# Top-32 attention with a highway layer behind it: the first pair of score tiles handled one tile at a time, and the order of the last instructions changed

## The chip, the cores and the metric

The kernel runs on one core of a Trainium2 chip. The metric is the device time of one execution in microseconds (us), as the median of several runs. The kernel before takes 830.66 us (five runs, 830.6 to 831.35).

## What is computed

For 8 batches and 8 heads, 576 queries meet 576 keys of width 64; each row of scores keeps its 32 largest, takes a softmax over them and weighs the values with it. The result goes through a highway layer of width 512.

```python
scores = scale * np.matmul(q, k.transpose(0, 1, 3, 2))
kth = np.partition(scores, -top_k, axis=-1)[..., -top_k:-top_k + 1]
scores = np.where(scores >= kth, scores, -1000000000.0)
attn = np.exp(scores - np.max(scores, axis=-1, keepdims=True))
x = np.matmul(attn / np.sum(attn, axis=-1, keepdims=True), v)   # then heads side by side: 4608 x 512
H = np.maximum(x @ w_h, 0.0)
T = 1.0 / (1.0 + np.exp(-(x @ w_t + b_t)))
return T * H + (1.0 - T) * x
```

## The kernel before

**Unit of work.** A tile is 128 query rows of one head by all 576 keys. Two tiles make a pair (a normal pair is the two heads 2i and 2i+1 of one block of queries), four pairs make a group (all heads of 128 queries), and 144 pairs make the kernel. The main loop (line 1016) takes one step `n` per pair; instructions are issued in the order in which they are written (the `Pinned` wrappers keep it), on PE (TensorE), DVE (VectorE), ACT (ScalarE), POOL (GpSimd) and the DMA queue of SP (SyncE). Since all instructions pass through those wrappers, the profile gives nearly all of them line 38, and they are told apart by the tiles that they write and read.

**One pair, from scores to output.** `scores` (line 222) multiplies queries by keys in fp32 into the PSUM tile `ps` of two tiles by 1024 columns. Columns 0 to 511 and 512 to 575 are separate products, and the products of the pair's two tiles alternate: tile 0 and tile 1 for the first 512 columns, then both for the last 64. The queries and keys of an even head lie in rows 0 to 63 of `kq`, those of an odd head in rows 64 to 127. There is one `ps`, so the scores of pair n+1 can be written only when the readers of pair n are through. `evac` (line 244) lets ACT write max(score, 0) of both tiles in one instruction of 1152 columns into an SBUF buffer (`zfirst` for pair 0, parts of `z0` to `z2` for the others). `tree` (line 255) has DVE fold the two halves of each row by a maximum into `hi`: for pairs 0 and 1 from the SBUF copy alone, later from `ps` and the copy, so that DVE then holds `ps` until it has read it. `folds` (line 275) folds on, into `hh`, `h3` and `w2`, `minima` (line 298) makes the folded-away smaller halves (DVE for pair 0, POOL for the others), and `lists`, `tops` and `rest` find the 32nd value of each row by rounds of MAX8 (eight largest) and MATCH_REPLACE8 (take them out). `run` issues such lists in rounds, one operation of each list per round. Later steps mask, transpose, take the exponential (`parts`), multiply by the values (`av`), and feed the finished group to the highway layer (`ffn_x`, `ffn_h`, `ffn_t` and so on).

**The opening.** Ahead of the loop, eight products of zeros keep PE going (`spin`, line 968). Then come the transposes of the first keys and of the first block of queries (`turn_first(pr, 0, 1)` for the first two heads), the scores of pair 0 and their evacuation, the transposes of the other six heads' first queries (`turn_first(pr, 1, NHP)`), whose copy into `kq` DVE makes (line 155, 384 columns), and the next keys, whose copy ACT makes. In step 0 DVE folds pair 0, and `run(opening, 1)` issues one round of its lists (line 1023). In step 1 PE computes the scores of pair 2, transposes the keys of pair 3, and then makes nine products of zeros (`WARM`, line 25). In step 2 it goes on with the scores of pair 3.

**The end.** After the loop (from line 1113) the last three pairs and the last two groups, `gp` and `gl`, are finished by an order written out by hand. `final_norm` divides the sums of heads by their denominators (DVE: RECIPROCAL into `scales`, then a product into `x`), `final_turn` transposes (PE) and copies to `xT` (DVE), `final_h` and `final_t` multiply by the two weights (PE), and `final_o` makes the last products and stores the two halves of the output (lines 650 to 665). In between stand the steps of the group before: `ffn_gate(gp)` (tanh on ACT), `ffn_e(gp)` (DVE, x times the gate, 512 columns), `ffn_o(gp)` (DVE, adds and stores, 512 columns) and `ffn_d(gl)` (DVE, 512 columns). `judge` looks whether the shortcuts held; a slow exact path behind it is not taken with these inputs.

Of the kernel before, what the change touches and what calls it, by code (L numbers as in the profile page):

```python
# [8 lines left out]
AF = mybir.ActivationFunctionType  # L9
# [12 lines left out]
NZ = 3  # L22
NPEN = 3
IDLE = {11: 3, 10: 8, 9: 3, 3: 3, 2: 3}
WARM = {1: 9, 2: 7, 3: 8}


class Pinned:


    def __init__(self, tc, engine):
        self._tc, self._engine = tc, engine
# [10 lines left out]
class PinnedCore:  # L43
    def __init__(self, tc):
        for name in ("tensor", "vector", "scalar", "gpsimd"):
            setattr(self, name, Pinned(tc, getattr(tc.nc, name)))
        self.sync = tc.nc.sync
        self.queue = Pinned(tc, tc.nc.sync)


class Group:
# [19 lines left out]
class Ops:  # L71


    def __init__(self, ctx, tc, shared, exact):
        self.tc = tc
        self.nc = tc.nc if exact else PinnedCore(tc)
        self.__dict__.update(shared)
        self.exact = exact
        s = "g" if exact else ""

        def pool(name, bufs, **kw):
            return ctx.enter_context(tc.tile_pool(name=name + s, bufs=bufs, **kw))

        PS = bass.MemoryType.PSUM
        self.ldpool = pool("ld", 2 if exact else 3)
        self.kqpool = pool("kq", 1 if exact else 2)
        self.scpool = pool("sc", 2) if exact else None
        self.treepool = pool("tree", 3)
        self.wpool = pool("w", 4)
        self.lpool = pool("l", 2)  # L90
        self.etpool = pool("et", 2)
        self.xpool = pool("x", 2)
        self.fpool = pool("f", 2)
        self.ztps = pool("ztps", 2, space=PS)
        self.zrps = pool("zrps", 1, space=PS)
        self.fps = pool("fps", 1, space=PS)
        self.bigctx = ctx.enter_context(ExitStack())
        self.bigps = self.bigctx.enter_context(
            tc.tile_pool(name="bigps" + s, bufs=1, space=PS)
        )  # L100
        self.st = {}
        self.quads = {}
        self.spare = []

    def load(self, pr, name, hp, eng=None, other=None, c0=0):
        nc, D, P = self.nc, self.D, self.P
# [35 lines left out]
    def turn_first(self, pr, h0, h1):  # L144


        nc, P = self.nc, self.P
        kqps = self.ztps.tile([P, 512], FP32, tag="zt", name="kqps")
        for hp in range(h0, h1):
            nc.tensor.transpose(  # L150
                kqps[:, hp * P : (hp + 1) * P],
                pr["qc"][:, 2 * hp : 2 * hp + 2, :].rearrange("p h d -> p (h d)"),
                self.ident[:],
            )
        nc.vector.tensor_copy(
            pr["kq"][:, 1, h0:h1, 0:P],
            kqps[:, h0 * P : h1 * P].rearrange("p (h q) -> p h q", q=P),
        )
# [63 lines left out]
    def scores(self, n, g, pi, prep):  # L222
        nc, D, S, P = self.nc, self.D, self.S, self.P
        kq = prep["kq"]
        qs = g.qt * P
        ps = self.bigps.tile([P, 2, 1024], FP32, tag="big", name="ps")
        for s0, s1 in ((0, 512), (512, S)):
            for ti, heads in enumerate(g.pairs[pi]):
                for hi, h in enumerate(heads):
                    r = slice((h % 2) * D, (h % 2 + 1) * D)  # L230
                    rows = slice(hi * (P // 2), hi * (P // 2) + g.qlen)
                    nc.tensor.matmul(
                        ps[rows, ti, s0:s1],
                        kq[r, 1, h // 2, qs : qs + g.qlen],
                        kq[r, 0, h // 2, s0:s1],
                    )
        self.st[n] = dict(ps=ps)

    def zview(self, n):
        if n == 0 and not self.exact:  # L240
            return self.zfirst
        return self.zbufs[n // 2 % NZ][:, 2 * (n % 2) : 2 * (n % 2) + 2, :]

    def evac(self, n):
        nc, P, S = self.nc, self.P, self.S
        ps = self.st[n]["ps"]
        if self.exact:
            sc = self.scpool.tile([P, 2, S], FP32, tag="sc", name="sc")
            nc.scalar.copy(sc[:], ps[:, :, 0:S])
        else:  # L250
            sc = self.zview(n)[:, :, 0:S]
            nc.scalar.activation(sc, ps[:, :, 0:S], AF.Relu)
        self.st[n]["sc"] = sc

    def tree(self, n):
        nc, P, S = self.nc, self.P, self.S
        H1, H2, H3 = S // 2, S // 4, S // 8
        k, half = n // 2, slice(2 * (n % 2), 2 * (n % 2) + 2)
        if n % 2 == 0 or n == 1:
            self.quads[n if n < 2 else k + 1] = tuple(  # L260
                self.treepool.tile([P, 4, w], FP32, tag=name, name=name, bufs=bufs)[
                    :, 0 : 2 if n < 2 else 4, :
                ]
                for name, w, bufs in (("hi", H1, 3), ("hh", H2, 3), ("h3", H3, 2))
            )
        ps, sc = self.st[n].pop("ps"), self.st[n]["sc"]
        if n < 2:
            hi, ps = self.quads[n][0], sc
        else:
            hi = self.quads[k + 1][0][:, half, :]  # L270
        nc.vector.tensor_tensor(
            hi[:, 0:2, :], ps[:, :, 0:H1], sc[:, :, H1:S], ALU.max
        )
# [24 lines left out]
    def minima(self, k, after):  # L298


        H1, H2 = self.S // 2, self.S // 4
        gp, S = self.nc.gpsimd, self.S
        hi, hh, h3 = self.quads[k]
        z = self.zview(k) if k < 2 else self.zbufs[(k - 1) % NZ]
        sci, hii, hhi = [a[:].bitcast(I32) for a in (z, hi, hh)]
        if k == 0:
            self.nc.vector.tensor_tensor(
                hi, z[:, :, 0:H1], z[:, :, H1:S], ALU.min
            )
            return  # L310
        if k == 1:
            head = gp.tensor_tensor(hii, sci[:, :, 0:H1], hii, ALU.subtract)
        else:
            head = gp.tensor_tensor(hhi, hii[:, :, 0:H2], hhi, ALU.subtract)
        self.tc.add_manual_dep(
            head.ins,
            after.ins.name,
            mybir.DependencyInfo(
                mybir.DependencyClass.Sync, mybir.DependencyReason.DATA
            ),  # L320
            reason="after the folds",
        )
        if k > 1:
            gp.tensor_tensor(hhi, hhi, hii[:, :, H2:H1], ALU.add)
            gp.tensor_tensor(hii, sci[:, :, 0:H1], hii, ALU.subtract)
        gp.tensor_tensor(hii, hii, sci[:, :, H1:S], ALU.add)
# [476 lines left out]
def kernel(  # L803
# [25 lines left out]
    def const(shape, dt, name):  # L829
        return consts.tile(shape, dt, tag=name, name=name)  # L830
# [8 lines left out]
    for i in range(NZ):  # L839
        zt = const([P, 4, nck * P], FP32, f"z{i}")  # L840
        nc.gpsimd.memset(zt[:, :, S : nck * P], NEG)
        zbufs.append(zt)
    zfirst = const([P, 2, nck * P], FP32, "zfirst")
    nc.gpsimd.memset(zfirst[:, :, S : nck * P], NEG)
    pens = []
    for i in range(NPEN):
        pt = const([P, 2, nck * P], BF16, f"pen{i}")
# [27 lines left out]
    with ExitStack() as cm:  # L875
# [100 lines left out]
        ops.load(pr, "qin", 2, queue, None, 1)  # L976
        ops.scores(0, *pairs[0], preps[0])
        ops.evac(0)
        ops.turn_first(pr, 1, NHP)
        ops.load_rest(pr, "qrest", queue, tag="qc")  # L980
        ops.turn(pr, "kin", 1, True)
# [30 lines left out]
        def values(m):  # L1012
            g, pi = pairs[m]
            ops.av(m, g, pi, preps[g.b]["vb"])

        while step <= NPR:
            n = step
            if have(n):
                ops.tree(n)
                if n < 2:  # L1020
                    ops.minima(n, ops.folds(n, *pairs[n], []))
                    opening += ops.lists(n, *pairs[n])
                    ops.run(opening, 1)
                elif n % 2:
                    nq = n // 2 + 1
                    ops.minima(nq, ops.folds(nq, *pairs[n - 1], fill))
                    fill = []
                if NHP <= n + 1 < 2 * NHP:
                    ops.turn(pr, "qin", n + 1 - NHP, None, 1)
                if n == NHP:  # L1030
                    ops.load(pr, "qin", 3, None, None, 1)
                if n == 2 * NHP:
                    ops.turn_rest(pr, 0, NHP, ("qrest",))
# [122 lines left out]
        part(1)  # L1156
        values(m + 1)
        ops.final_norm(gl, 2, 3)
        ops.ffn_gate(gp)
        ops.ffn_e(gp)  # L1160
        gl.ps = ops.fps.tile([P, 512], FP32, tag="fp", name="hps")
        ops.final_h(gl, 0, 2)
        values(m + 2)
        ops.final_turn(
            gl, 2, 3, ops.ztps.tile([P, 512], FP32, tag="zt", name="xtps")
        )
        ops.final_norm(gl, 3, 4)
        ops.final_t(gl, 0, 2)
        judge(banks[3])
        ops.final_turn(  # L1170
            gl, 3, 4, ops.ztps.tile([P, 512], FP32, tag="zt", name="xtps")
        )
        ops.ffn_o(gp, *out_rows(gp))
        ops.final_h(gl, 2, 3)
        ops.final_t(gl, 2, 3)
# [79 lines left out]
```

## Time and profile before

| | |
|---|---|
| median of five runs | 830.66 us |
| the profiled execution | 831.33 us |
| its span, first to last instruction | 829.6 us |
| DVE busy | 814.7 us |
| ACT busy | 761.6 us |
| PE busy | 710.8 us |
| POOL busy | 710.7 us |
| last instruction of DVE ends | 825.05 us |
| mean granted clock of TensorE | 0.989 |

The profile is that of one execution, and its times count from the start of the span. An instruction's row gives its start, its length, the engine, the tile that it writes and the tile that it reads, and, in brackets, how long the engine had been idle and what ended that. Instructions on one engine overlap a little: a row's length is longer than the distance to the next row. The chain of waits is the work that ended last, followed back from the last instruction.

### The profile page before, as it was taken

What the parts mean: (1) busy time and instruction counts of PE and PEld (TensorE: products, weight loads), DVE (VectorE), ACT (ScalarE), POOL (GpSimd) and SP (SyncE); (2) the same over time, 40 slices, a digit from 0 to 9 for tenths busy, and PEclk for the clock granted to TensorE, in tenths of its full rate; (3) what the DMA queues carried; (4) which work ended last, traced back from release to release, by engine and by line L of the source; (5) the groups of instructions that cost most, each with busy time, mean ns of one, the idle gap of its engine ahead of it and who ended that gap; (6) DMA issues with size and microseconds to landing.
All of it is one profiled execution on the core that took longest, in us unless ns stands there. A gap on an engine that the chain in (4) does not pass through costs nothing.

```text
span 829.6 us, 20251 instructions
## 1 busy us (share of the span) xinstructions
PE 710.8 (86%) x6635; PEld 490.2 (59%) x6635; DVE 814.7 (98%) x4173; ACT 761.6 (92%) x1522; POOL 710.7 (86%) x460
## 2 busy tenths in 40 slices
PE   8788888788898888888888898878988888899986
PEld 4565566565566656665566565656556655565654
DVE  5999999999999999999999999999999999999997
ACT  4899999999999999899999999989999999988985
POOL 5888888798889889978889988888888989887993
PEclk9999999999999999999999999999999999999999
DMA  8564333234254431433325342323413321111222
GB/s 187 131 109 84 65 90 75 61 68 90 38 102 84 77 90 30 75 71 65 90 53 92 70 96 58 64 53 71 112 31 65 52 40 40 40 36 25 45 39 56
DMA packets 105329, 58.40 MB, mean 70 GB/s; under 512 B 82304, under 2 KB 91904, under 8 KB 105216
## 3 DMA queue, kind: packets, MB, share of 16 engines
q1 hardware_dynamic: 93200, 37.47, 17.6%
q0 software_dynamic: 11200, 19.27, 16.2%
q8 instruction: 54, 0.88, 0.4%
q14 instruction: 59, 0.48, 0.2%
q10 hardware_dynamic: 816, 0.30, 0.1%
HBM read 30.67 MB, written 18.35 MB: 59 GB/s over the span
## 4 chain that ended last, share of the span: by engine, by line
DVE 94%; PE 3%; ACT 1%; POOL 1%; issue 0%; POOLq 0%; DVEq 0%
DVE w L38 53%; DVE m L38 20%; DVE hi L38 11%; DVE hh L38 6%; DVE h L38 3%; PE warm L38 1%; PE ps L38 1%; PE zt L38 1%; PE t L38 1%; DVE scales L38 0%; POOL hh L38 0%; ACT pen L38 0%; POOL hi L38 0%; ACT z L38 0%; ACT kq L38 0%
## 5 line engine op out<-in xcount | busy, mean ns | idle before, releaser
L38 PE MATMUL ps<-kq 64*128 64x64 f32 (+3 forms) x1280 | 202.3, 439 | 47.7 <-DVE hi L38 42.4
L38 ACT ACTIVATE pen<-z,m 128x576 bf16<-128x576 f32 x286 | 225.7, 790 | 1.2 <-DVE m L38 1.0
L38 PE MATMUL zt<-ident,z 128*128 128x128 f32 x1140 | 212.5, 280 | 2.0 <-ACT xT L38 2.0
L38 PE MATMUL zt<-nident,pen 128*128 128x128 bf16 x1148 | 205.7, 220 | 0.0
L38 ACT ACTIVATE z<-ps 128x1152 f32<-128x1152 f32 x143 | 161.9, 1132 | 43.1 <-PE ps L38 39.3
L38 POOL TENSOR_TENSOR hi<-z,hi 128x1152 int32<-128x1152 int32 (+1 forms) x72 | 188.3, 2616 | 11.2 <-DVE hh L38 5.6
L38 POOL TENSOR_TENSOR hi<-hi,z 128x1152 int32<-128x1152 int32 (+1 forms) x72 | 189.9, 2638 | 5.6
L38 PEld LDWEIGHTS ps<-kq 64*128 64x128 f32 (+1 forms) x1280 | 102.8, 176 | 143.7 <-issue 80.1
L38 PEld LDWEIGHTS zt<-ident,z 128*128 128x128 f32 x1140 | 161.1, 141 | 16.5 <-ACT xT L38 2.9
L38 ACT ACTIVATE et<-zt 128x512 bf16<-128x512 f32 x287 | 162.1, 601 | 5.6 <-PE zt L38 1.7
L38 POOL TENSOR_TENSOR hh<-hi,hh 128x576 int32<-128x576 int32 x71 | 104.5, 1472 | 71.4 <-DVE w L38 71.3
L38 PEld LDWEIGHTS <-pen 128*128 128x128 bf16 x1440 | 152.2, 106 | 15.8 <-ACT pen L38 10.4
L38 DVE MAX8 m<-w 128x8 f32<-128x168 f32 x576 | 158.9, 315 | 0.0
L38 PE MATMUL zr<-v,et 128*128 128x65 bf16 (+1 forms) x1590 | 98.2, 196 | 44.5 <-ACT et L38 36.9
L38 PEld LDWEIGHTS <-et 128*128 128x128 bf16 (+1 forms) x1600 | 69.2, 101 | 85.1 <-ACT et L38 82.2
L38 DVE MAX8 w<-hi 128x8 f32<-128x288 f32 x288 | 115.6, 441 | 0.1
L38 POOL TENSOR_TENSOR hh<-hh,hi 128x576 int32<-128x576 int32 x71 | 100.4, 1414 | 5.6
L38 DVE TENSOR_TENSOR hi<-ps,z 128x576 f32<-128x576 f32 x142 | 104.4, 735 | 0.5 <-ACT z L38 0.5
L38 DVE MAX8 w<-hh 128x8 f32<-128x72 f32 x576 | 96.4, 217 | 0.0
L38 DVE MATCH_REPLACE8 w<-m,w 128x168 f32<-128x168 f32 x288 | 88.6, 313 | 0.0
L38 PE MATMUL zr<-ident,z 128*128 128x128 f32 x284 | 67.5, 291 | 7.1 <-ACT xs L38 7.1
L38 ACT ACTIVATE x<-xs,scales 128x64 f32<-128x64 f32 x272 | 68.2, 336 | 0.0
(106 smaller groups left out, 1187.2 us busy)
## 6 DMA issues: line engine op xcount, KB each, us to landing
x<-d POOLq DMA_DIRECT2D x35, 256.0 KB, 3.9
vin<-in_v_dram SPq DMA_DIRECT2D x8, 1024.0 KB, 5.5
kin<-in_k_dram SPq DMA_DIRECT2D x63, 128.0 KB, 3.4
out_dram<-d SPq DMA_DIRECT2D x31, 256.0 KB, 2.3
out_dram<-t POOLq DMA_DIRECT2D x30, 256.0 KB, 4.2
qin<-in_q_dram SPq DMA_DIRECT2D x56, 128.0 KB, 3.0
qrest<-in_q_dram SPq DMA_DIRECT2D x8, 128.0 KB, 3.4
vrest<-in_v_dram SPq DMA_DIRECT2D x8, 128.0 KB, 3.0
```

What stands on the lines that cost most here:

```text
L38: return self._tc.keep_in_program_order(fn(*args, **kw))
```

## The change

Five things are changed.

1. **Pair 0, tile by tile.** Its scores go into two PSUM tiles of their own (a pool `firstps`, closed behind the evacuation, so that `bigps` opens in its place), all products of tile 0 first and then those of tile 1. The copy `zfirst` becomes two buffers. ACT evacuates in two instructions of 576 columns, and DVE makes the first maximum and the first minimum of the fold in two instructions each (288 columns of output).
2. **Query copies.** The copy of the other six heads' first queries (384 columns) goes from DVE to ACT, behind the evacuation of pair 0.
3. **Rounds.** Step 0 issues three rounds of the lists of pair 0 in place of one.
4. **Products of zeros.** In step 1 there are five in place of nine.
5. **The end.** `ffn_gate(gp)` moves behind the sums of the last pair (`values(m + 2)`), the last `final_norm(gl, 3, 4)` moves ahead of the turn of block 2, and `ffn_e(gp)` moves behind the turn of block 3.

```diff
-WARM = {1: 9, 2: 7, 3: 8}
+WARM = {1: 5, 2: 7, 3: 8}
...
+class Halves:
+    def __init__(self, tiles, width):
+        self.tiles, self.width = tiles, width
+
+    def __getitem__(self, key):
+        p, ti, cs = key
+        return self.tiles[ti][:, 0 : self.width][p, cs]
...
-        nc.vector.tensor_copy(
+        copy = nc.scalar.copy if h0 else nc.vector.tensor_copy
+        copy(
             pr["kq"][:, 1, h0:h1, 0:P],
...
-        ps = self.bigps.tile([P, 2, 1024], FP32, tag="big", name="ps")
-        for s0, s1 in ((0, 512), (512, S)):
-            for ti, heads in enumerate(g.pairs[pi]):
+        spans = ((0, 512), (512, S))
+        order = [(s, ti) for s in spans for ti in (0, 1)]
+        if n == 0 and not self.exact:
+            ps = Halves(
+                [
+                    self.bigps.tile([P, 1024], FP32, tag=f"f{ti}", name="ps")
+                    for ti in (0, 1)
+                ],
+                1024,
+            )
+            order = [(s, ti) for ti in (0, 1) for s in spans]
+        else:
+            ps = self.bigps.tile([P, 2, 1024], FP32, tag="big", name="ps")
+        for (s0, s1), ti in order:
+            for heads in (g.pairs[pi][ti],):
...
+        elif n == 0:
+            sc = Halves(self.zfirst, S)
+            for ti in (0, 1):
+                nc.scalar.activation(sc[:, ti, :], ps[:, ti, 0:S], AF.Relu)
...
+        if n == 0:
+            for ti in (0, 1):
+                nc.vector.tensor_tensor(
+                    hi[:, ti, :], ps[:, ti, 0:H1], sc[:, ti, H1:S], ALU.max
+                )
+            return
...
+        if k == 0:
+            for ti in (0, 1):
+                self.nc.vector.tensor_tensor(
+                    hi[:, ti, :], z[:, ti, 0:H1], z[:, ti, H1:S], ALU.min
+                )
+            return
...
         ops.evac(0)
+        ops.open_big("bigps")
         ops.turn_first(pr, 1, NHP)
...
-                    ops.run(opening, 1)
+                    ops.run(opening, 1 + 2 * (n == 0))
...
         ops.final_norm(gl, 2, 3)
-        ops.ffn_gate(gp)
-        ops.ffn_e(gp)
         gl.ps = ops.fps.tile([P, 512], FP32, tag="fp", name="hps")
         ops.final_h(gl, 0, 2)
         values(m + 2)
+        ops.ffn_gate(gp)
+        ops.final_norm(gl, 3, 4)
         ops.final_turn(
             gl, 2, 3, ops.ztps.tile([P, 512], FP32, tag="zt", name="xtps")
         )
-        ops.final_norm(gl, 3, 4)
         ops.final_t(gl, 0, 2)
         judge(banks[3])
         ops.final_turn(
             gl, 3, 4, ops.ztps.tile([P, 512], FP32, tag="zt", name="xtps")
         )
+        ops.ffn_e(gp)
         ops.ffn_o(gp, *out_rows(gp))
```

Apart from these, the order of the instructions on PE, DVE, ACT, POOL and SP is the same as before, with one thing that follows from the rounds: the two lists of pair 1 that were cut in two around the maximum of pair 3 (two MAX8 pairs behind it) are now finished ahead of it.

More of the change, by code (lines that the diff above doesn't have):

```diff
@@ L97, in __init__ @@
         self.bigctx = ctx.enter_context(ExitStack())
-        self.bigps = self.bigctx.enter_context(
-            tc.tile_pool(name="bigps" + s, bufs=1, space=PS)
-        )
+        self.open_big("bigps" if exact else "firstps")
         self.st = {}
@@ L103, in __init__, with open_big @@
         self.spare = []
+    def open_big(self, name):
+        self.bigctx.close()
+        self.bigps = self.bigctx.enter_context(
+            self.tc.tile_pool(name=name, bufs=1, space=bass.MemoryType.PSUM)
+        )
     def load(self, pr, name, hp, eng=None, other=None, c0=0):
@@ L240, in zview @@
         if n == 0 and not self.exact:
-            return self.zfirst
+            return Halves(self.zfirst, self.zfirst[0].shape[-1])
         return self.zbufs[n // 2 % NZ][:, 2 * (n % 2) : 2 * (n % 2) + 2, :]
@@ L304, in minima @@
         z = self.zview(k) if k < 2 else self.zbufs[(k - 1) % NZ]
-        sci, hii, hhi = [a[:].bitcast(I32) for a in (z, hi, hh)]
[L306 to L310, printed above, removed]
+        if k == 0:
+            for ti in (0, 1):
+                self.nc.vector.tensor_tensor(
+                    hi[:, ti, :], z[:, ti, 0:H1], z[:, ti, H1:S], ALU.min
+                )
+            return
+        sci, hii, hhi = [a[:].bitcast(I32) for a in (z, hi, hh)]
         if k == 1:
@@ L842 @@
         zbufs.append(zt)
-    zfirst = const([P, 2, nck * P], FP32, "zfirst")
-    nc.gpsimd.memset(zfirst[:, :, S : nck * P], NEG)
+    zfirst = [const([P, nck * P], FP32, f"zf{i}") for i in (0, 1)]
+    for zt in zfirst:
+        nc.gpsimd.memset(zt[:, S : nck * P], NEG)
     pens = []
```

## The prediction, made before the changed kernel ran

> **What bounds the kernel.** First the page: busy shares, and the chain that ended last.
>
> ```profile
> PE 710.8 (86%) x6635; PEld 490.2 (59%) x6635; DVE 814.7 (98%) x4173; ACT 761.6 (92%) x1522; POOL 710.7 (86%) x460
> ...
> DVE 94%; PE 3%; ACT 1%; POOL 1%; issue 0%; POOLq 0%; DVEq 0%
> ```
>
> DVE is the bound: 98% busy, 94% of the chain. The list of waits has DVE idle for only 9 us in all, 8.1 of them in the opening (0.9, 6.7 and 0.5 us) and 0.9 at the end. The change removes no DVE work from the stretch between, so it counts only by how early DVE becomes busy for good, and by what stands between DVE's last waits and the end. So I read these two places.
>
> The chain of waits, opening (start, us, what):
>
> ```profile
> 6.33 1.31 PE ps L38 x8
> 7.64 0.02 issue
> 7.66 1.13 ACT zfirst L38
> 8.79 0.48 ACT kq L38
> 9.28 0.04 issue
> 9.32 1.32 PE ps L38 x8
> ...
> 14.20 1.94 PE warm L38 x9
> 16.15 1.25 PE ps L38 x8
> 17.40 0.02 issue
> 17.42 1.14 ACT z L38
> 18.56 0.02 issue
> 18.58 0.76 DVE hi L38
> ```
>
> Scores, evacuation and key copy alternate three times, then come nine products of zeros and the scores of pair 3. DVE's fold of pair 3 at 18.58 is the last that waits for them (0.54 us idle). From there DVE is never idle. My yardstick is DVE's fold `h<-hh` of the pairs 2 and 3, at 20.47: what it gains, the kernel gains.
>
> The timeline of DVE, end:
>
> ```profile
> 819.33 0.17 DVE L38 RECIPROCAL scales<-xs 128x2 f32<-128x2 f32 x1 [0.43 <-ACT xs L38]
> 819.53 0.29 DVE L38 TENSOR_TENSOR x<-xs,scales 128x128 f32<-128x128 f32 x1
> 819.82 0.69 DVE L38 SCALAR_TENSOR_TENSOR x<-t,x 128x512 f32<-128x512 f32 x1
> 820.42 0.28 DVE L38 TENSOR_SCALAR xT<-xtps 128x128 bf16<-128x128 f32 x1
> 820.62 0.16 DVE L38 RECIPROCAL scales<-xs 128x2 f32<-128x2 f32 x1
> 820.81 0.29 DVE L38 TENSOR_TENSOR x<-xs,scales 128x128 f32<-128x128 f32 x1
> 821.59 0.29 DVE L38 TENSOR_SCALAR xT<-xtps 128x128 bf16<-128x128 f32 x1 [0.48 <-PE xtps L38]
> 821.96 0.69 DVE L38 SCALAR_TENSOR_TENSOR d<-x,d 128x512 f32<-128x512 f32 x1
> 822.57 0.69 DVE L38 SCALAR_TENSOR_TENSOR d<-hps,xh 128x512 f32<-128x512 f32 x1
> ```
>
> `ffn_e` (819.82) fills time in which DVE would wait for the last sums. `ffn_d` at 822.57 follows `ffn_o` by 0.61, as an independent step of 512 follows another (819.82 to 820.42): the end is DVE's, not PE's, whose product for it ends at 822.33.
>
> **Part 1, the scores of pair 0 in tile order: nothing gained, perhaps much lost.** In the timeline two `ps` passes start together at 6.33, two at 6.85, two at 7.28 and two at 7.33. A product is two passes (1280 records for 640 products), and in the program both passes of tile 0 stand ahead of those of tile 1. I read the pairs as tile 0 beside tile 1, on rows 0-63 and 64-127: a queue that lets tile 1's first pass go past tile 0's blocked second one. Weight loads agree: the first and second start within 0.02, the third 0.11 later. If it can also pass six blocked instructions in place of two, both tiles still end near 7.63 (forecast). If not, tile 1 starts only with tile 0's last passes, at 7.30, and takes 0.43 + 0.43 + 0.05 to its own last pass and 0.27 for that: 8.48, 0.85 later (rival A). If the passes that start together are the two of one product, tile 0 is done at about 7.1 and the total stays (rival B). For the forecast: in the second scores the sequencer must have taken all eight passes in by 9.55, where it executes the wait behind them, while the passes for 64 columns only start at 10.28; so some ten instructions can lie waiting.
>
> [...]
>
> **Part 2, evacuation in halves, query copy on ACT.** Copies of 512 take 0.58 and of 1152 1.13, so 576 take 0.64, the next starting 0.53 later. Halves at 7.62 and 8.16 end at 8.26 and 8.80 (before: 8.79). The copy of 384 columns (0.48, taking 0.38 of ACT's time) now stands ahead of the key copy, so the second scores start at 9.70, not 9.32. DVE's copy (0.56 at 8.14) cost nothing where it was: DVE was waiting.
>
> **Part 3, DVE.** The second half of the first maximum starts at 8.83, `hh` a dependent step of 288 later (0.49, as 9.62 to 10.11): 9.32, not 9.62. To the first MAX8 it was 2.22; the minimum in two halves (0.36 each for 0.67) makes it 2.28: 11.60. MAX8 pair 0.28, then the two rounds brought forward (0.41 and 0.28): the fold of pair 1 starts at 12.57 (was 12.12). Its data are ready at 11.79 + 0.38 = 12.17. The same 2.89 as before gives the fold of pair 2 at 15.46; its data come at 14.79 + 0.38 = 15.17.
>
> [...]
>
> **Part 4, fewer zeros.** Four products of 0.216 leave PE's path. PE is through at 14.20 + 0.38 + 5 x 0.216 = 15.66. But the scores of pair 3 need `ps`, which DVE's fold of pair 2 holds until 15.46 + 0.74 = 16.20: this wait takes the place of the zeros. They start at 16.24 (was 16.15 in the chain, 16.08 in the timeline). From 16.08 to the fold at 18.58 it was 2.50: now 18.74. Behind the waiting scores on PE stand only zeros and the next query transposes; the fourth scores start at 19.89 for a fold at 24.66, over 3 us of cover.
>
> DVE is done with everything else by 15.46 + 0.65 + 2.22 = 18.33 (five MAX8 pairs, two MATCH_REPLACE8 pairs) and idles 0.4. Two MAX8 pairs that stood between the folds now stand ahead, but the folds then depend directly on each other: 0.78 twice (as 12.12 to 12.90), so `h` starts at 20.30. **Opening: -0.17.**
>
> **Part 5, the end.** The last sums leave PE at 819.87 and ACT's copy ended at 820.18; ACT was free at 819.79, so moving the tanh wins nothing. RECIPROCAL 820.22, product 820.41 to 820.70 (0.40 earlier). PE is busy until `judge` ends at 820.98, then transposes 0.30: the last `xT` at 821.36, not 821.59. DVE has idled 0.40 ahead of the RECIPROCAL and 0.47 ahead of this. Now `ffn_e` follows, at 821.66 (0.30: between 0.20 for an independent step and the 0.37 that `ffn_o` needed with its many DMA waits), `ffn_o` a dependent step later (0.79, as 822.57 to 823.36), 822.45, `ffn_d` at 823.06, not 822.57. Behind it the order is the same, the tanh of `gl` (822.53) is covered, and the last store goes as much later. **End: +0.49**, between 0 (if something else already sets `ffn_d`) and 0.69 (all of `ffn_e`).
>
> POOL only gets one more memset (0.2 us) ahead of 5.6 us of idling; SP's queue issues the same DMAs.
>
> **Sum.** -0.17 + 0.49 = +0.32 on the profiled execution's 831.33 (span 829.6 and 1.73 around it): 831.65. That execution lies 0.67 above the median of the runs shown, so **831.0** as a median.
>
> **Rivals.**
> A, *the tiles run one after the other* (slower than before). Scores end 0.85 later; the second half is evacuated by 9.15, `hh` at 9.67, fold of pair 2 at 15.81, scores of pair 3 at 16.59, `h` at 20.65: +0.18, with the end +0.67: 831.3. It decides if the queue passes fewer than six blocked instructions. For it: nothing in the trace passes more than two. Against: the ten that lie waiting.
> B, *tile 0 done at half time* (faster). Halves at 7.13 and 7.66, `hh` at 8.82, second scores at 9.20, fold of pair 2 at 14.96, `h` at 19.80: -0.67, with the end -0.18: 830.5. For it: equal starts alone don't say which pass is whose. Against: four passes for 512 columns would take 0.43 a product where all-bf16 products of 512 take 0.22 each.
> C, *the clock*: with fewer zeros PE drops to half clock. It did from 27.1 to 30.5, after 1.55 us busy of 3.4. At 10.0 to 13.4 it was busy for 2.28 and kept its clock; the new stretch has about as much. If it falls, the scores of the pairs 2 and 3 take 0.96 us more each (their passes, 0.43 twice and 0.05 twice, doubled), less 0.29 that the fold of pair 2 has to spare: about +1.7 on the forecast, 832.7. It decides from a busy share between those two.
>
> **Numbers.** Forecast 831.0: 0.55; A 831.3: 0.23; B 830.5: 0.15; C 832.7: 0.04; anything else 0.03. A run of this kernel can be told from no change at about 0.2% (1.7 us), and of the cases only C passes that: faster 0.02, within 0.93, slower 0.05. The range takes in B with an end that costs nothing (829.99) and A with the dearest end (831.5), and 0.1 to 0.2 for the scatter of the runs: 829.9 to 831.7.
>
> **What would show it.** Scores of pair 0: two passes starting together and an end near 7.7 (forecast), a span near 2.1 us (A), or a first half evacuated from 7.1 (B). Second scores at 9.7, 10.1 or 9.2. Those of pair 3 waiting for DVE's `hi`, not for zeros. At the end, idling ahead of the second RECIPROCAL and `ffn_d` later by half a microsecond against the sums. I am wrong if DVE's last steps stay where they were, or if DVE shows new idle time between 25 and 815.

## The result, and the profile after

The changed kernel takes **831.74 us** (median of 26 runs, 830.59 to 833.07); the kernel before 830.66 us (46 runs, 829.91 to 831.47). The ratio is 1.0013, 95% interval 1.0008 to 1.0019: 1.1 us slower, within the 0.2% that the prediction called no change, but 0.04 us beyond the upper end of its range and 0.7 above its forecast.

Two things about these runs carry all that follows. The profiled executions differ by far less than the medians (831.51 against 831.33, spans of 829.8 and 829.6 us). And the runs of the changed kernel, its profiled ones included, form two groups with a gap from 831.75 to 832.21: 15 runs with a mean of 831.24 and 13 with a mean of 832.47. Those of before form one group (standard deviation 0.34). So there is a small loss in every execution, and a larger one in about half of them, and the first profile is one of the better group.

The chain of waits of the changed kernel, opening (start, us, what):

```profile
6.33 1.29 PE ps L38 x5
7.62 0.02 issue
7.64 1.20 ACT zf L38 x2
...
15.59 0.67 DVE hi L38
16.25 0.14 issue
16.39 1.31 PE ps L38 x8
17.70 0.02 issue
17.72 1.14 ACT z L38
18.86 0.02 issue
18.88 0.77 DVE hi L38
19.65 0.02 issue
19.67 0.77 DVE hh L38
20.44 0.02 issue
20.47 0.46 DVE h L38
```

The yardstick's row in the timeline of DVE, in the kernel before and then in the changed one:

```profile
20.47 0.44 DVE L38 TENSOR_TENSOR h<-hh 128x288 f32<-128x288 f32 x1
```

```profile
20.47 0.46 DVE L38 TENSOR_TENSOR h<-hh 128x288 f32<-128x288 f32 x1
```

The scores run from 6.33 and the first half is evacuated from 7.64: tile 0 is not ready early (rival B), and tile 1, whose last pass ends at 7.75, is not late by 0.85 (rival A). The zeros are gone from the chain; DVE's hold of `ps` stands in their place, and 0.14 us pass between DVE's end and PE's start. The fold of pair 3 comes at 18.88 (before: 18.58), but the fold `h<-hh`, the yardstick, starts at 20.47 in both kernels. The opening is worth 0.00. The other profiles agree: from the start of the first scores to the yardstick it is 14.14 to 14.15 us in all seven with the whole new opening, and 14.15 to 14.23 in eight of the nine with the whole old one (14.52 in the ninth, four_idle_steps).

The timeline of DVE, end, same kernel:

```profile
819.30 0.17 DVE L38 RECIPROCAL scales<-xs 128x2 f32<-128x2 f32 x1 [0.43 <-ACT xs L38]
...
820.18 0.17 DVE L38 RECIPROCAL scales<-xs 128x2 f32<-128x2 f32 x1 [0.40 <-ACT xs L38]
...
821.24 0.29 DVE L38 TENSOR_SCALAR xT<-xtps 128x128 bf16<-128x128 f32 x1 [0.36 <-PE xtps L38]
821.46 0.69 DVE L38 SCALAR_TENSOR_TENSOR x<-t,x 128x512 f32<-128x512 f32 x1
822.18 0.69 DVE L38 SCALAR_TENSOR_TENSOR d<-x,d 128x512 f32<-128x512 f32 x1
822.79 0.68 DVE L38 SCALAR_TENSOR_TENSOR d<-hps,xh 128x512 f32<-128x512 f32 x1
...
824.83 0.42 DVE L38 TENSOR_TENSOR o<-d,x 128x256 f32<-128x256 f32 x1
```

DVE's last step before:

```profile
824.62 0.43 DVE L38 TENSOR_TENSOR o<-d,x 128x256 f32<-128x256 f32 x1
```

PE's rows ahead of the last `xT`, in the changed kernel (the end of `judge` and the last transposes):

```profile
820.76 0.19 PE L38 MATMUL t<-ones,bad 128*1 128x1 f32 x2
820.88 0.33 PE L38 MATMUL xtps<-ident,x 128*128 128x128 f32 x1
```

The last `xT` is 0.35 us earlier than before, and three steps of 512 columns stand behind it in place of two. From the first RECIPROCAL shown to the last step of DVE (which ends at 825.25, before at 825.05) it takes 5.95 us, 0.23 more than before. That is the difference of the two spans.

### The profile page after: what moved, and what is told of

It is laid out like the page before. It is cut to its first block, busy times and chain, and to the rows that moved or that the text cites. A ratio compares the mean times of both kernels' runs of the same rounds, so it can differ in the third digit from the quotient of the medians.

```text
span 829.8 us, 20246 instructions
## 1 busy us (share of the span) xinstructions
PE 710.2 (86%) x6631; PEld 490.1 (59%) x6631; DVE 814.5 (98%) x4174; ACT 762.0 (92%) x1524; POOL 710.8 (86%) x461
## 4 chain that ended last, share of the span: by engine, by line
DVE 95%; POOL 2%; PE 1%; issue 1%; ACT 0%; DVEq 0%; POOLq 0%
DVE w L38 53%; DVE m L38 20%; DVE hi L38 11%; DVE hh L38 6%; DVE h L38 3%; POOL hi L38 1%; POOL hh L38 1%; DVE scales L38 0%; PE warm L38 0%; PE ps L38 0%; DVE ok L38 0%; DVE d L38 0%; POOL t L38 0%; ACT zf L38 0%; DVE x L38 0%
```

## The experiments

All kernels of a group ran on one chip beside the kernel before. Means and standard deviations are of all runs shown (11 with the profiled one, 6 for four_idle_steps).

### Which part carries the wide scatter?

**end_only**: the kernel before with the new order of the end (part 5) and nothing else. **opening_only**: the changed kernel with the old end. **before_5_zeros** and **after_9_zeros** exchange one number:

```diff
-WARM = {1: 9, 2: 7, 3: 8}
+WARM = {1: 5, 2: 7, 3: 8}
```

> The kernel before with the new order at the end alone. The two profiled executions differ by 0.2 us in span (829.6 and 829.8), the medians by 1.08 us. Theory of the sums (what the two profiles show is all there is, the rest of the medians' difference is chance): the end alone gives +0.2 us, 830.9, with the scatter of the kernel before. Theory of the zeros (with five products of zeros in place of nine PE drops to half clock at a bad place in some executions, and these lift the median): +0.2 us, and no more scatter than before, since the zeros are not touched. Theory of the end (the later gate product meets something that comes late in some executions, its DMA or the store behind it): +0.9 to +1.1 us and a wide scatter, 830.6 to 833.

> The changed kernel with the end of before. Theory of the sums: the fold of the pairs 2 and 3 starts at 20.47 in both profiles, so 0.0 us, 830.7, scatter as before. Theory of the zeros: +0.7 to +0.9 us, with a scatter as wide as that of the changed kernel (830.6 to 833.1), and some executions with a lower mean clock among the long ones. Theory of the end: 0.0 us, narrow scatter.

> The kernel before with five products of zeros in step 1 in place of nine, nothing else. In its profile the scores of pair 3 should start at about 15.8 instead of 16.08, since DVE holds ps until 15.75: -0.3 us by the chain, 830.4. Theory of the sums and theory of the end: that, with the scatter of before. Theory of the zeros: the median goes up instead, by 0.5 us or more, and the scatter widens to over 2 us.

> The changed kernel with nine products of zeros again. In its profile PE is through with the zeros at about 16.5 (14.53 + 9 x 0.216), the scores of pair 3 start at 16.5 instead of 16.39: +0.1 us by the chain. Theory of the sums: as the changed kernel or 0.1 us slower, within 0.3 of the kernel before. Theory of the zeros: the median falls to 830.9 to 831.0 and the scatter to that of before, though the chain in the profile is no shorter. Theory of the end: 831.7 to 831.8 and a wide scatter, as the changed kernel.

Measured (before: 831.26, deviation 0.22):

| kernel | median | mean | deviation | ratio, 95% interval |
|---|---|---|---|---|
| end_only | 831.65 | 832.01 | 0.75 | 1.0011 [1.0002, 1.0020] |
| opening_only | 831.66 | 831.50 | 0.57 | 1.0004 [0.9995, 1.0013] |
| before_5_zeros | 831.20 | 831.21 | 0.35 | 1.0000 [0.9991, 1.0009] |
| after_9_zeros | 831.78 | 832.00 | 0.72 | 1.0010 [1.0001, 1.0019] |

The theory of the zeros falls: without them before stays as it was (the 0.3 us that its expectation read off the chain were not gained either), and with them the changed kernel scatters as wide as ever, while its yardstick comes 0.27 us later (14.41 us behind the first scores, not 14.14). Three of the eleven runs of end_only lie 1.7 to 2.0 us over before, so the new end alone can bring late runs. But opening_only scatters too (0.57, without a gap), and its median is as high: this group alone does not tell the two parts apart. All four profiles were of runs that were not late, so they could not show the cause.

### Which step of the end?

**norm_only** moves the norm (first diff), **late_gate_product** the gate product (second diff; the tanh stays); **opening_and_norm** is opening_only with the norm's move; **after_again** is the changed kernel once more.

```diff
+        ops.final_norm(gl, 3, 4)
         ops.final_turn(
             gl, 2, 3, ops.ztps.tile([P, 512], FP32, tag="zt", name="xtps")
         )
-        ops.final_norm(gl, 3, 4)
```

```diff
         ops.ffn_gate(gp)
-        ops.ffn_e(gp)
...
+        ops.ffn_e(gp)
         ops.ffn_o(gp, *out_rows(gp))
```

> The kernel before with one edit: the last norm (RECIPROCAL and product) stands ahead of the turn of block 2, as in the changed kernel; the tanh and the gate product of the group before stay where they were. Theory of the sums: the gate product still fills the wait for the last sums, the last norm comes 0.2 earlier (820.42 and not 820.62), PE's last transposes follow, the last xT is at 821.40 and not 821.59, and the end comes 0.2 us earlier than before: ratio 0.9998, nothing that a median can tell, and no wider scatter. Theory of the late product: the scatter that the new end showed (some executions 1.3 to 2 us late) needs the gate product behind the last xT; so here the runs lie as close together as those of before (deviation 0.2 to 0.35 us). Rival, theory of the norm: the scatter comes with the norm's new place; then some of these runs lie 1.3 us or more above the median of before.

> The kernel before with one edit: the gate product of the group before stands behind the turn of block 3; the tanh and the norms stay where they were. Theory of the sums: DVE waits for the last sums without cover, and the product of 0.6 us comes behind the last xT; the last xT is at about 821.2 to 821.3 (the turn of block 2 and the norm no longer wait for the product), the three long steps follow, and the last one is 0.2 to 0.4 us later than before: ratio 1.0003 to 1.0005. Theory of the late product: about a quarter of the runs lie 1.3 to 2 us above the median of before, as with the whole new end. Rivals: theory of the norm, or of the tanh's new place: no such runs here, a deviation of 0.2 to 0.35 us.

> The changed kernel's opening and, of its end, only the norm's new place; tanh and gate product as before. Theory of the sums: the opening gives 0 to -0.3, the norm -0.2: a median 0.2 to 0.5 us under before (ratio 0.9994 to 0.9998). With less idle time for DVE the end can wait for the accumulating transfer that POOL issues for the gate product (4.2 to 5.2 us from issue to landing in the profiles so far): where it lands later than 819.8, the gate product shows a wait for a DMA and the gain is gone. If the opening by itself widens the scatter, as it seemed to, the deviation is 0.5 us or more here too; if not, 0.35.

> The changed kernel once more, on this chip, beside the others. If its median shift of about 1 us belongs to the kernel and not to the chip on which it was first timed, this run shows 831.7 to 831.9 against some 831.2 of before (ratio 1.0005 to 1.0015) and a deviation of 0.5 to 0.8 us, twice that of before; a second profile shows whether its opening and its end repeat to 0.1 us (first scores from 6.33 to 7.75, the yardstick at 20.5, the last sums' RECIPROCAL at 820.2 with a wait of 0.4). If the profile is that of a late execution (832.3 or more), the place where DVE or the transfers are late shows the cause.

Measured (before: 830.68, deviation 0.34): norm_only 830.32 (deviation 0.25, ratio 0.9999 [0.9990, 1.0008]); late_gate_product 832.28 (0.81, 1.0014 [1.0005, 1.0023]); opening_and_norm 830.98 (0.32, 1.0004 [0.9995, 1.0014]; 0.2 to 0.5 under before had been expected); after_again 831.69 (0.73, 1.0013 [1.0004, 1.0022]). The gate product alone brings the two groups (five runs up to 831.51, six from 832.28); the moves of norm and tanh are not needed for them.

And two of these profiles, late_gate_product and after_again, are of late executions. In after_again DVE's last step ends at 824.68, 0.57 earlier than in the first profile, and yet the span ends at 830.6 and not 829.8. The lost time lies behind the last instruction of DVE: 5.9 us from there to the end of the span, against 4.5 in the first profile and in before. The transfers from 822 on (bytes, median us from issue to landing), first in the first profile of the changed kernel, then in after_again:

```profile
out_dram<-o SPq DMA_DIRECT2D x1, 128.0 KB, 2.0
out_dram<-o ACTq DMA_DIRECT2D x1, 128.0 KB, 2.0
```

```profile
out_dram<-o SPq DMA_DIRECT2D x1, 128.0 KB, 2.0
out_dram<-o ACTq DMA_DIRECT2D x1, 128.0 KB, 3.9
```

In before ACT's store landed in 2.2 us:

```profile
out_dram<-o ACTq DMA_DIRECT2D x1, 128.0 KB, 2.2
```

Only the very last store, that of ACT's queue, is late, by 1.9 us. Its 144 packets are on queue q10. These are the transfers of after_again from 825.5 to 826.2 and then from 826.2 to 828.1 (packets, MB, share of the 16 engines):

```profile
q10 hardware_dynamic: 135, 0.12, 51.5%
q8 instruction: 1, 0.02, 12.9%
```

```profile
q10 hardware_dynamic: 9, 0.01, 2.7%
```

135 packets start within 0.5 us; the other 9 start one after another from 827.28 on. Nine is one sixteenth of 144, and the profile counts 16 DMA engines; the trace does not name a packet's engine, so that the nine share one is the author's conclusion from their number. Between the 135 and the nine lies one packet of 16 KB on q8, a **fetch of instructions**, that started at 825.87 and took 1.45 us, to 827.32. In the first profile the store's window, 826.0 to 826.7, holds 141 packets and none of q8:

```profile
q10 hardware_dynamic: 141, 0.13, 55.5%
q14 instruction: 1, 0.01, 4.8%
```

In before all 144 lie between 825.9 and 826.6, again without one of q8 (q1 carries SP's stores):

```profile
q10 hardware_dynamic: 144, 0.13, 55.4%
q1 hardware_dynamic: 7, 0.01, 2.5%
```

In the first profile of the changed kernel the fetch started at 826.72, with the store's last packet; in before at 827.03, 0.5 us behind it. Over the profiles that were undisturbed it starts as the store's last packet does or up to 0.9 us later; in the late ones it starts some 0.3 us behind the first packet.

What sends for it? In all profiles up to here (but for opening_and_norm, where it is 2.6) a first fetch on q8 starts 1.95 to 2.02 us behind the start of DVE's last `xT`, and a second, the one in question, 3.1 to 3.5 (once 4.3) behind the first. The last `xT` is what PE's last products wait for; behind these, in the program, PE branches over the exact path. So the fetch seems to hang on PE's end, and the last store on DVE's. In the old end the store is issued 3.5 us behind the start of the last `xT` (821.59 to 825.08), in the new one 4.05 (821.24 to 825.29). That half microsecond moves the store into the fetch. And why only in some executions? In the five profiles up to here with the gate product behind the last `xT` the store's first packet starts 4.89 to 4.91 us behind that `xT`; the second fetch starts 5.15 and 5.20 behind it in the two late ones, and 5.44 to 5.48 in the three others, as the store's last packets do. So a quarter of a microsecond in the fetch's place tells the two groups apart; what makes that difference is not shown.

### Is it the fetch?

**after_pe_held** has `spin(4, banks[3])` behind PE's last product. **two_idle_steps** and **four_idle_steps** leave the old end as it is and put two or four DVE steps whose output is not used behind the last `xT` (the diff has two); **norm_and_sum_ahead** is norm_only with `ffn_o(gp)` ahead of the turn of block 3.

```diff
+        za = zbufs[0]
+        for _ in range(2):
+            vec.scalar_tensor_tensor(
+                out=za[:, 1, 0:512], in0=za[:, 0, 0:512], scalar=1.0,
+                in1=za[:, 0, 0:512], op0=ALU.max, op1=ALU.min,
+            )
         ops.ffn_o(gp, *out_rows(gp))
```

> The changed kernel with four more products of zeros behind PE's last product, ahead of its branch over the exact path. They are on nobody's path. Theory of the fetch: in the late executions the last store of the output (ACT's queue) lands 3.9 us after its issue and not 2.0 to 2.2, because a 16 KB fetch of instructions (queue 8, some 4.5 to 4.8 us behind PE's last product, 1.0 to 1.7 us long) gets to one of the 16 DMA engines ahead of the store's packets on it; with PE's branch 0.9 us later, the fetch comes behind the store in every execution. No run is late: the runs lie within 1.3 us of one another (deviation 0.2 to 0.35), the median is 0.1 to 0.4 above before (ratio 1.0001 to 1.0005), 0.7 to 1 us less than the changed kernel's. The profile shows the last store landing in 2.0 to 2.3 us and the second late fetch on queue 8 behind the store's last packet. Rival, the scatter comes from the steps on DVE or from the store before: half of the runs stay 1.3 to 1.7 us above the others, as in the changed kernel.

> The kernel before, with two DVE steps of 128x512 that compute nothing of use (a maximum and a minimum over a score buffer, into that buffer), behind the last xT, ahead of the last sum and everything that stands behind it. They cost DVE 0.6 us each. Theory of the fetch: the last store's packets move 1.2 us later, wholly into the fetch that follows PE's branch, so that nearly every run is late: before plus 1.2 plus 0.5 to 1.2 us (ratio 1.0020 to 1.0029), and the profile shows the last store landing in 2.7 to 3.5 us. Rival (the lateness comes with the place of the gate product itself): before plus 1.2 us (ratio 1.0014), all runs close together, the last store landing in 2.0 to 2.3 us.

> The same with four such steps, 2.4 us of DVE. Theory of the fetch: the last store now comes behind the fetch and is disturbed no more: before plus 2.4 us (ratio 1.0029), all runs close together (deviation 0.2 to 0.4), the last store landing in 2.0 to 2.3 us; so the second pair of steps costs only 0 to 0.7 us more than the first, although it is 1.2 us of DVE work on the path. Rival (lateness grows with what stands behind the last xT): two pairs cost the same each, or runs late by 1.7 us remain.

> The kernel before with the last norm ahead of the turn of block 2, and in addition the last sum of the group before (128x512 on DVE) ahead of the last xT, where DVE waited 0.29 us for PE; the gate product stays where it was before. Theory of the sums: the last xT is 0.3 us later, the three steps behind it have become two, and DVE ends 0.2 to 0.3 us earlier than with the norm alone, 0.4 to 0.6 earlier than before; the store of the group before goes out 0.6 us earlier. Theory of the fetch: PE's branch comes 0.3 later and the last store 0.25 earlier, which is away from the collision: no late runs. So a median 0.4 to 0.7 us under before (ratio 0.9992 to 0.9995). Rival: PE's last products, 0.3 us later with the xT, end behind the sum and set the last steps, and nothing is gained over the norm alone.

Measured (before: 830.72, deviation 0.25): two_idle_steps 832.68, deviation 0.36, ratio 1.0022 [1.0013, 1.0031]; four_idle_steps 833.52, 0.37, 1.0032 [1.0020, 1.0044]. As the theory of the fetch has it: the first two steps cost 1.96 us for 1.2 us of DVE work, the next two only 0.84 (0 to 0.7 expected), and ACT's store lands in 3.5 us in the one and 2.1 in the other.

after_pe_held was a miss: 831.83, deviation 0.88, as many late runs as ever. Its profile, itself of a late execution, shows why:

```profile
822.00 1.03 PE L38 MATMUL t<-idle 128*128 128x512 bf16 x4
```

The zeros run to 823.03, but the first fetch still starts at 823.24, 2.04 behind the start of the last `xT` (821.20), as without them. So the fetch does not follow the end of PE's work. If it follows PE's sequencer, that must go on past products which wait for nothing; to move the fetch, it must be made to wait.

norm_and_sum_ahead: 830.47 (deviation 0.25, 0.9998 [0.9989, 1.0007]). No late runs, but nothing over the norm alone: DVE now idles 0.54 us ahead of `ffn_d`, which starts at 821.98, 0.10 behind the end of PE's product for it (821.88): the rival of its expectation. (The profile names POOL's queue as the releaser.) Its first fetch is 2.54 us behind the last `xT`, as late as that of opening_and_norm; why in these two, is open.

### PE's sequencer made to wait

In these four a product of one column, its result unused, stands behind PE's last product and reads what DVE has just written; after_pe_waits and end_pe_waits (end_only with it) have

```diff
         ops.final_t(gl, 3, 4)
+        ops.nc.tensor.matmul(
+            banks[3][0:1, 0:1], gp.x[:, 0:1], ones[:], start=True, stop=True
+        )
```

two_idle_pe_waits (two_idle_steps with it) reads `za[:, 1, 0:1]`, and in after_pe_waits_longer the product stands in `final_o`, behind the first half of the output, and reads `o[:, 0:1]`.

> The changed kernel with one small product more on PE (one column by one column, its result unused) behind PE's last product, which reads what the gate product of the group before has written on DVE, so that PE's sequencer waits 0.6 us longer ahead of its branch. Theory of the fetch: in the kernels so far PE's first late 16 KB fetch came 2.0 us behind the start of the last xT, the second 3.2 to 3.5 behind that, and the second meets the last store's packets (4.9 to 5.5 us behind the xT here, 4.4 to 5.0 in the old end). 0.6 later, the second comes at 5.8 to 6.1, behind the store: no late runs, deviation 0.2 to 0.4, a median 0.1 to 0.5 above before (ratio 1.0001 to 1.0006), and the last store lands in 2.0 to 2.3 us. Rival, the fetch only follows from something else that is late: two groups of runs remain, 1.3 us apart, median shift 1 us.

> The kernel before with the new end alone and the same small product on PE. Theory of the fetch: no late runs, a median 0.1 to 0.3 above before, which is the 0.2 of DVE's later end; what the changed kernel with this product costs beyond that is the opening's. Rival: a quarter of the runs 1.3 to 2 us late, as with the new end alone.

> The kernel before with two idle DVE steps of 128x512 behind the last xT, in which nearly all runs were late (1.96 us over before for 1.2 us of DVE), and a small product on PE that waits for the second of them, so that PE branches 1.3 us later. Theory of the fetch: the second fetch comes at 6.4 to 6.8 us behind the xT, the store's packets at 5.5 to 6.1: only the 1.2 us remain (ratio 1.0013 to 1.0017), the last store lands in 2.0 to 2.3 us. Rival: before plus 2.0, as without the product.

> The changed kernel with a small product on PE that waits for the first half of the output (DVE's o), so that PE branches some 2.9 us later. Theory of the fetch: now PE's first late fetch comes at about 4.9 us behind the last xT, right onto the last store's packets (4.9 to 5.5): nearly all runs are late, 1 to 1.7 us over the changed kernel's better group, and the last store lands in 3 to 4 us. If one product that waits for a little is right and one that waits for long is wrong, it is the time of the fetch that counts and not the product. Rival: a later branch can only help, or does nothing: the runs are as with the shorter wait.

Measured (before: 830.56, mean 830.53, deviation 0.23):

| kernel | median | mean | deviation | ratio, 95% interval | first, second fetch at | last store lands in |
|---|---|---|---|---|---|---|
| after_pe_waits | 830.79 | 830.74 | 0.25 | 1.0003 [0.9994, 1.0012] | 822.71, 826.40 | 2.4 us |
| end_pe_waits | 830.99 | 830.91 | 0.35 | 1.0005 [0.9996, 1.0015] | 822.76, 826.50 | 2.5 us |
| two_idle_pe_waits | 831.78 | 831.73 | 0.28 | 1.0014 [1.0005, 1.0024] | 824.37, 827.99 | 2.4 us |
| after_pe_waits_longer | 831.82 | 831.90 | 0.27 | 1.0016 [1.0007, 1.0025] | 825.22, 829.00 | 3.9 us |

PE's rows in after_pe_waits and in after_pe_waits_longer:

```profile
821.04 0.19 PE L38 MATMUL t<-ones,x 128*1 128x1 f32 x2
```

```profile
823.61 0.19 PE L38 MATMUL t<-ones,o 128*1 128x1 f32 x2 [2.41 <-DVE o L38]
```

The transfers of after_pe_waits from 824.9 to 826.0, then those of after_pe_waits_longer from 825.1 to 825.8:

```profile
q10 hardware_dynamic: 144, 0.13, 35.4%
q1 hardware_dynamic: 14, 0.02, 4.1%
q14 instruction: 1, 0.01, 1.8%
```

```profile
q10 hardware_dynamic: 135, 0.12, 52.6%
q8 instruction: 1, 0.02, 14.9%
```

In each of these kernels the first fetch starts 1.61 to 1.75 us behind this product, wherever it stands: the fetch follows PE's wait. (The branch over the exact path comes next in the program; that it is what sends for the fetch was the author's assumption, and no row shows it.) With a short wait both fetches miss the store (packets from 824.91 to 825.98) and no run is late. With a long one the first fetch meets the store (from 825.15 on), and every run of the one lies above every run of the other (831.50 and up against 831.03 and down; means 831.90 and 830.74). DVE takes the same time in both (its last step starts 3.58 and 3.59 us behind the start of the last `xT`), and both have the product; only the time of the fetch differs. The same product takes 0.7 us from two_idle_steps (each kernel against before on its own chip) and leaves the 1.2 us of its DVE steps. This settles the cause.

Three details were not as expected: with the product the second fetch comes 3.6 to 3.8 us behind the first, not 3.1 to 3.5; where both fetches miss, the last store still lands in 2.4 to 2.5 us, not 2.0 to 2.3; and end_pe_waits lies 0.4 over before, not 0.1 to 0.3.

## Why the prediction was wrong

- **Part 1, scores in tile order: right.** The first half is evacuated from 7.64 (forecast 7.62); tile 1's passes run some 0.14 behind tile 0's and end at 7.75. A and B are refuted. In the program tile 0's four passes stand first, but the trace starts four passes of 512 columns (6.33, 6.46, 6.85, 6.99) ahead of the four of 64 (7.28, 7.33, 7.42, 7.48): tile 1's go past tile 0's, and rival A's order does not hold for these two tiles. The eight take 1.42 us, where four of 0.43 one after another would take 1.72 alone.
- **Parts 2 and 3: right to 0.05 us.** Second scores 9.75 (9.70), first MAX8 11.65 (11.60), fold of pair 1 12.61 (12.57), fold of pair 2 15.50 (15.46).
- **Part 4: the mechanism right, the size off.** The wait for DVE's hold takes the place of the zeros. PE started 0.14 behind DVE's end, not at once, and the yardstick came at 20.47, not 20.30: 0.00 for -0.17. In before_5_zeros, too, the fold of pair 3 comes 12.25 us behind the start of the first scores, as before. The clock (rival C) did not fall there: the granted clock is 1.00 in every stretch from 6 to 23.7 us, before and after.
- **Part 5 on DVE: right in kind, too dear.** The steps behind the last `xT` start at 821.46, 822.18 and 822.79 (forecast 821.66, 822.45, 823.06). PE's last transposes started at 820.88 and did not wait for `judge` to end (at 820.95), so the last `xT` came at 821.24, not 821.36; the gate product followed it by 0.22, not 0.30, and the next step by 0.72, not 0.79. +0.23 for +0.49. The errors of parts 4 and 5 have opposite signs, so that their sum, +0.32, is near the +0.2 of the profile is partly luck. after_pe_waits, in which the fetch is out of the way, lies 0.21 over before by the means: what the profile's rows say, +0.2, is the price of the change without the fetch.
- **The step that failed** is the sentence at the end of part 5: "Behind it the order is the same, the tanh of `gl` (822.53) is covered, and the last store goes as much later." It took the store's landing as a fixed delay behind its issue. Moved by half a microsecond against PE's end, the store met the fetch that comes behind PE's last products, in about half of the executions, and each of those lost some 1.2 to 1.4 us (15 and 13 runs, 831.24 and 832.47; 5.9 us and 4.5 from DVE's last step to the span's end). That is the 0.8 us between the changed kernel and after_pe_waits, as ratios 1.0013 and 1.0003. No rival named it, and the range, made of the openings and the ends on DVE, did not hold it. The trace of before had these fetches too, and its numbers would have shown the danger: there the second fetch starts 5.44 us behind the last `xT` and the store's last packet at 826.52. With the prediction's own shifts (`xT` at 821.36, the store 0.49 later) that is 826.80 and 827.01: the fetch among the packets. The median is only 0.04 us outside the range, but what moved it there stood in no term of the sum.
- **The offset** of 0.67 between the profiled execution and the median was taken as it stood, and that was fair to the kernel before. It could not carry over to a kernel with two groups of runs.

**What stays open.** Why the means of the runs set the opening's worth between -0.17 (after_pe_waits against end_pe_waits) and +0.45 (opening_and_norm against norm_only), when the yardstick says 0.00 in profile after profile. Why two of eleven runs of opening_only, with the old end, reached 832.1 and 832.3: no profile of such a run was taken, but in the one that there is the second fetch starts at 826.31, already among the store's last packets (up to 826.37), so that a hit is not far there either. And what sets the fetch's place from one execution to the next. No kernel here beats the one before by more than can be told; norm_only and norm_and_sum_ahead (0.9999 and 0.9998) come closest.

## What to carry to other kernels

The span did not end with the last instruction of DVE: it went on for 4.5 us in the first profile of the changed kernel, and for 5.9 in after_again, whose last store took 1.9 us longer to land. So read the DMA queues behind the last busy row as well, and ask which transfers start there by another engine's clock, as the instruction fetch did here. Moving work from ahead of a wait to behind it lengthens the distance between one engine's end and another's, and that can matter more than the work: here the distance from the last `xT` to the store's issue grew from 3.5 to 4.05 us, DVE's end came 0.2 us later, and the executions in which the store met the fetch lost 1.2 to 1.4. When runs fall into two groups, one profile shows one group: profile again until the other is seen, before explaining a median.

## What the runs showed of the hardware

- **An instruction fetch held up a store.** In the five late profiles one fetch packet of 16 KB took 1.4 to 1.7 us, nine packets of the store (135 came ahead of them in after_again and in after_pe_waits_longer) started only as it ended, and the whole store landed late (3.5 to 4.0 us; 2.0 to 2.2 in before and in the first profile of the changed kernel). The fetches came when PE had no product left to do (in the first profile its last product ended at 822.20, and they started at 823.21 and 826.72), and in the late executions another engine's store, that of ACT's queue, paid for one of them.
- **The first fetch followed PE's wait, not the end of its products.** Four products of zeros (1.03 us) behind the last product moved the fetch from 1.97 to 2.04 us behind the last `xT` (after_pe_held); a product that waited for DVE moved it to 2.71 with the short wait (after_pe_waits) and to 4.98 with the long one (after_pe_waits_longer).
- **PE started 0.14 us after the end of the DVE instruction that released it** (16.25 to 16.39 in the changed kernel; in before, 0.14 ahead of the transpose at 821.25), in the chain's "issue".
- **The profiled executions ran at two paces, the same kernel at both.** From `h<-hh` at 20.47 to the first RECIPROCAL of the end it was 798.83 us in the first profile of the changed kernel and 798.25 in after_again, same code. After 422.6 us of it the difference is 0.27 us, at the end 0.58 (0.07%), so it grew on the way. Of the 18 profiles (the kernels before and after and the 16 runs), nine lie at 798.74 to 798.88 and nine at 798.16 to 798.34. Both kinds have late and undisturbed executions, so the pace is not what makes a run late. The start of the first scores varies as well, from 5.66 to 6.33 us; the two together are wide enough for most of the scatter of an undisturbed kernel, which was not tested further.
